# Attention and phase mixing on one core: one PSUM tile, finer loads and phase steps, a new order of all steps

## Chip, core and metric

One core of a Trainium2 chip. The metric is the device time of one execution in microseconds (us); less is better. Steps are issued in a hand-given order, and each engine (PE for products, DVE, ACT and POOL for elementwise work, SP for plain transfers) takes its instructions in that order.

## The reference, cut to what matters

```
scores = q @ k.T / sqrt(64), masked          # 4 batches, 8 heads, 768 positions, 64 wide
                                             # heads 0,2,6: causal; others: 4 sinks + window of 64
x      = softmax(scores) @ v                 # heads side by side: x is (4, 768, 512)
theta  = x @ w_theta
y      = w_tok_r @ (x*cos(theta)) + w_tok_i @ (x*sin(theta))   # over positions, per batch
u      = x + y
out    = u + max(u @ w_ch, 0)
```

## The kernel before

The program is the text `ORDER` (line 54): 732 steps, each a name with arguments, run one after the other by the table `run` (line 435). The framework puts in the waits from the program order and from what the steps read and write; within one engine the order is that of the text.

Per batch b: `lq` (line 206) has POOL load all of q or all of k into `qb`/`kb` as bf16; batch 0 comes through `lf` (line 201, SP) by pair of heads and is cast by `cf`. `tq` (line 225) turns a pair with six (batch 0) or twelve transposes on PE, `eq` copies the result out of PSUM into `qT`/`kT`. `s` (line 254) makes scores of one of 17 units, mostly two halves of up to 512 columns in two PSUM banks; `e` (line 299) is one exponential on ACT over both banks; `m` masks in SBUF on DVE. `av` (line 350) multiplies with v, `n` (line 365) divides on DVE and gives x. x is turned by PE and a copy in batch 0 (`xp`, `xe`), by a transposing transfer on SP later (`xd`). `th` (line 395) makes theta of two row blocks at once, `tr` (line 401) takes cosine and sine of it on ACT into `ct`/`st`, `z` (line 406) multiplies x by one of them: part r mostly both blocks in one DVE instruction of 1024 columns (y = 2), part i one block each, on DVE or POOL. `mx` (line 413) adds four products to the bank of one of six output blocks; three `mx` with p = 0, 1, 2 in that order complete a block. `u` adds x, `ud` turns u by a transfer, `ch` (line 424) makes the last product, `o` (line 428) finishes, `st` stores.

PSUM is four tiles of two banks (line 144). A step that needs one bank gets half of a tile (`one`), a step that needs two gets a whole tile (`two`), so that the two banks of a pair always begin at an even number. `ct`/`st`, `u`, `ot` and the loaded blocks `wtok` take their buffers round robin by their own number. `gv` (line 213) is a small DVE copy that holds the loads of v back.

```
banks = [psum.tile([128, 2, 512], F32, name=f"bank{n}") for n in range(4)]   # line 144
```

Of the kernel before, what the change touches and what calls it, by code (L numbers as in the profile page):

```python
# [57 lines left out]
tq.0.q.3.1 ko.0.1.D lq.1.k sv.0.D e.0.1.4 s.0.6.2 cv.0.1.D lq.1.q eq.0.q.3.1.D eq.0.k.3.0.A s.0.7.4 lw.t e.0.7.4 m.0.1 s.0.5.0 cv.0.2.D lt.0.0 e.0.5.0
m.0.12 s.0.4.4 e.0.6.2 s.0.15.0 bv.0.2.D lt.0.1 m.0.7 e.0.2.6 m.0.5 s.0.3.2 ko.0.3.P m.0.6 e.0.4.4 s.0.14.6 lt.1.0 m.0.2 cv.0.3.D bv.0.0.A lt.1.1
s.0.16.4 m.0.4 e.0.14.6 lt.2.0 cv.0.4.D e.0.16.4 s.0.9.6 bv.0.4.D lt.2.1 e.0.9.6 s.0.8.4 m.0.16 bv.0.3.P e.0.8.4 s.0.13.6 m.0.9 e.0.3.2 m.0.8 e.0.13.6  # L60
m.0.3 tq.1.k.0.4 tq.1.k.3.5 bv.0.1.A m.0.13 av.0.1.2 eq.1.k.0.4.A av.0.2.6 n.0.1.2 eq.1.k.3.5.A tq.1.k.2.4 e.0.15.0 n.0.2.6 av.0.3.2 eq.1.k.2.4.A
ko.1.3.D tq.1.k.1.5 n.0.3.2 cv.0.5.A xp.0.1.0 lq.2.k xp.0.2.1 av.0.0.6 xe.0.1.0.A m.0.15 xp.0.3.4 eq.1.k.1.5.A n.0.0.6 ko.1.2.P av.0.5.2 xe.0.3.4.A
ko.1.1.P tq.1.q.2.0 xe.0.2.1.A n.0.5.2 tq.1.q.0.4 eq.1.q.2.0.A xp.0.0.5 eq.1.q.0.4.D tq.1.q.1.1 xe.0.0.5.A av.0.4.6 eq.1.q.1.1.A xp.0.5.0 n.0.4.6
th.0.0.2 xe.0.5.0.A wt.0.0.0 tq.1.q.3.1 lt.3.0 th.0.1.4 eq.1.q.3.1.D lq.2.q tr.0.0.2 wt.1.0.1 wt.1.1.6 wt.0.1.7 we.1.0.1.A we.1.1.6.D z.0.0.i.0.P
wt.2.0.2 xp.0.4.3 we.0.1.7.D tr.0.1.4 xe.0.4.3.D wt.2.1.1 we.2.0.2.D lt.3.1 th.0.2.6 z.0.0.i.1.D lt.4.0 z.0.0.r.2.D we.0.0.0.A lt.4.1 we.2.1.1.A
s.1.13.2 z.0.1.r.2.D lt.5.0 s.1.1.4 mx.0.0.0.0 tr.0.2.6 z.0.1.i.1.P z.0.1.i.0.D mx.0.2.0.1 lt.5.1 mx.0.0.1.0 z.0.2.r.2.D z.0.2.i.1.P s.1.9.6
mx.0.2.1.1 e.1.1.4 lw.c e.1.9.6 z.0.2.i.0.P m.1.1 s.1.12.4 e.1.12.4 m.1.9 wt.3.0.6 mx.0.0.2.0 e.1.13.2 m.1.12 we.3.0.6.A s.1.8.4 m.1.13 s.1.16.2
mx.0.2.2.1 u.0.0.0 e.1.8.4 ud.0.0 s.1.7.6 e.1.16.2 u.0.2.1 s.1.5.0 tq.2.q.3.4 m.1.8 e.1.5.0 tq.2.q.2.5 ud.0.2 e.1.7.6 s.1.2.2 m.1.16 wt.3.1.0 gv.1
tq.2.k.1.1 m.1.5 e.1.2.2 lv.1.2 we.3.1.0.D s.1.4.6 eq.2.q.3.4.A m.1.7 lv.1.0 s.1.0.2 tq.2.q.1.0 lv.1.5 e.1.0.2 m.1.2 mx.0.1.0.4 lv.1.1 lv.1.3 e.1.4.6
m.1.0 s.1.11.2 lv.1.4 mx.0.1.1.4 e.1.11.2 m.1.4 s.1.6.6 mx.0.1.2.4 e.1.6.6 wt.5.0.2 cv.1.2.A u.0.1.4 wt.4.1.3 s.1.15.6 bv.1.2.P lv.2.2 we.5.0.2.D  # L70
we.4.1.3.A tq.2.k.2.4 m.1.6 ud.0.1 tq.2.k.3.2 e.1.15.6 mx.0.3.0.3 eq.2.k.2.4.D cv.1.0.A wt.5.1.6 eq.2.k.3.2.D eq.2.q.2.5.A ko.2.2.P lv.2.0 mx.0.3.1.3
we.5.1.6.A bv.1.0.P sv.1.D ko.2.3.P s.1.3.4 m.1.15 mx.0.3.2.3 e.1.3.4 s.1.14.6 cv.1.5.A u.0.3.3 mx.0.5.0.2 eq.2.q.1.0.A lv.2.5 m.1.3 ud.0.3
eq.2.k.1.1.A av.1.0.4 cv.1.1.D mx.0.5.1.2 n.1.0.4 e.1.14.6 lv.2.1 ko.2.1.P av.1.1.0 bv.1.1.D xd.1.0 mx.0.5.2.2 n.1.1.0 av.1.2.4 cv.1.3.D xd.1.1
u.0.5.2 ch.0.2.3 bv.1.3.A cv.1.4.D lv.2.3 av.1.3.6 n.1.2.4 bv.1.4.P lv.2.4 wt.4.0.2 ud.0.5 o.0.2.3 s.1.10.0 we.4.0.2.A ch.0.1.4 n.1.3.6 xd.1.2
e.1.10.0 mx.0.4.0.5 o.0.1.4 xd.1.3 av.1.4.2 st.0.1 st.0.2 av.1.5.6 n.1.4.2 ch.0.3.4 cv.2.0.A n.1.5.6 xd.1.4 cv.2.5.A bv.2.0.P mx.0.4.1.5 cv.2.1.D
xd.1.5 sv.2.P o.0.3.4 th.1.0.0 cv.2.2.D lv.3.1 st.0.3 lv.3.5 bv.2.2.P mx.0.4.2.5 lv.3.0 cv.2.3.P cv.2.4.D lv.3.2 bv.2.1.P ch.0.0.4 lv.3.3 u.0.4.5
bv.2.4.P tr.1.0.0 lv.3.4 bv.2.3.P ch.0.5.2 o.0.0.4 ud.0.4 th.1.1.6 o.0.5.2 st.0.0 st.0.5 z.1.0.r.2.D z.1.0.i.1.P tq.2.q.0.0 tr.1.1.6 z.1.0.i.0.D
tq.2.k.0.1 lq.3.q th.1.2.4 eq.2.k.0.1.D lq.3.k eq.2.q.0.0.A z.1.1.i.1.D z.1.1.i.0.P mx.1.0.0.1 tr.1.2.4 z.1.1.r.2.D s.2.7.2 s.2.0.6 s.2.5.0 mx.1.0.1.1
z.1.2.r.2.D z.1.2.i.1.P mx.1.1.0.4 mx.1.2.0.5 z.1.2.i.0.P e.2.7.2 mx.1.1.1.4 e.2.5.0 m.2.7 e.2.0.6 mx.1.2.1.5 m.2.5 m.2.0 mx.1.1.2.4 s.2.10.2 u.1.1.4
s.2.11.6 e.2.10.2 mx.1.2.2.5 ud.1.1 e.2.11.6 mx.1.0.2.1 u.1.2.5 ud.1.2 s.2.9.2 u.1.0.1 s.2.4.4 e.2.9.2 s.2.13.6 mx.1.3.0.0 ud.1.0 e.2.4.4 m.2.9  # L80
mx.1.5.0.1 e.2.13.6 m.2.4 mx.1.3.1.0 m.2.13 mx.1.5.1.1 s.2.8.2 mx.1.3.2.0 e.2.8.2 s.2.3.4 u.1.3.0 s.2.2.6 s.2.1.2 e.2.3.4 mx.1.5.2.1 m.2.8 ud.1.3
# [427 lines left out]
```

## Time and profile before

| what | us |
|---|---|
| median of 3 runs (lowest, highest) | 209.87 (208.6, 210.0) |
| span of the profiled execution, first to last instruction | 208.0 |
| PE busy, share of the span | 170.2, 82% |
| DVE busy | 137.7, 66% |
| ACT busy | 123.7, 59% |
| POOL busy | 55.8, 27% |

The profiled execution has no time of its own beside its span; the runs are 0.6 to 2.0 us above the span. An engine's busy time counts each instruction from start to modelled end, so products that overlap in the pipeline make PE look fuller than it is: its pace is read from how many products start in a stretch.

### The profile page before, as it was taken

How to read it: one execution, taken by the hardware profiler on the slowest of the kernel's cores; microseconds unless marked ns; L12 is line 12 of the kernel's file. 1: busy time of each engine (PE TensorE's matmuls, PEld its weight loads, DVE VectorE, ACT ScalarE, POOL GpSimd, SP SyncE). 2: the span in 40 equal slices, each digit the busy share in tenths (PEclk: the TensorE clock that was granted, in tenths of full speed). 3: DMA queues.
4: the chain of work that ended last, by engine and by line, in shares of the span. 5: the costliest groups of instructions: out<-in, count | busy, mean ns of one | idle time of the engine just before them, and what ended most of it. 6: DMA issues, size and time to landing. Idle time of an engine off the chain costs nothing.

```text
span 208.0 us, 4245 instructions
## 1 busy us (share of the span) xinstructions
PE 170.2 (82%) x1707; PEld 94.0 (45%) x1728; DVE 137.7 (66%) x255; ACT 123.7 (59%) x147; POOL 55.8 (27%) x80
## 2 busy tenths in 40 slices
...
GB/s 196 340 225 156 199 205 208 171 92 202 145 95 196 187 157 159 208 174 186 188 173 199 110 31 127 159 87 50 15 54 111 50 129 150 34 71 76 58 144 151
DMA packets 61938, 29.49 MB, mean 142 GB/s; under 512 B 48096, under 2 KB 58848, under 8 KB 61920
## 3 DMA queue, kind: packets, MB, share of 16 engines
...
## 4 chain that ended last, share of the span: by engine, by line
PE 46%; DVE 20%; DMA 12%; ACT 12%; issue 5%; SPq 2%; POOL 0%; DVEq 0%; ACTq 0%; POOLq 0%
PE bank L416 19%; DMA uT<-u 8%; PE bank L426 8%; ACT P L306 5%; PE bank L363 5%; DVE u L422 4%; PE bank L276 4%; PE bank L399 4%; DMA early<-in_q_dram 3%; DVE ot L429 3%; PE bank L232 3%; DVE kT L238 2%; DVE zr L411 2%; DVE early L411 2%; ACT kT L236 2%
## 5 line engine op out<-in xcount | busy, mean ns | idle before, releaser
L306 ACT ACTIVATE P<-bank 128x1024 bf16<-128x1024 f32 (+2 forms) x64 | 57.3, 948 | 15.5 <-PE bank L276 15.5
L426 PE MATMUL bank<-w_ch_sb,uT 128*128 128x512 bf16 x91 | 23.8, 379 | 5.6 <-DMA uT<-u 1.8
L416 PE MATMUL bank<-zr,wtokTr 128*128 128x512 bf16 x67 | 25.5, 381 | 3.5 <-DVE zr L411 1.1
L328 DVE TENSOR_TENSOR P<-P,m_stream 128x1024 bf16<-128x1024 bf16 (+3 forms) x36 | 21.0, 587 | 10.1 <-ACT P L306 9.8
L416 PE MATMUL bank<-early,wtokTi 128*128 128x512 bf16 x71 | 26.9, 379 | 0.3 <-issue 0.2
L276 PE MATMUL bank<-qT,kT 64*128 64x128 bf16 (+3 forms) x240 | 23.0, 271 | 4.7 <-DVE kT L238 1.7
L416 PE MATMUL bank<-early,wtokTr 128*128 128x512 bf16 x68 | 25.7, 379 | 1.1 <-ACT qT L236 0.4
L416 PE MATMUL bank<-zi,wtokTi 128*128 128x512 bf16 x69 | 26.1, 379 | 0.5 <-issue 0.3
L429 DVE SCALAR_TENSOR_TENSOR ot<-bank,u 128x512 f32<-128x512 f32 x24 | 16.1, 687 | 14.5 <-PE bank L416 6.8
L416 PEld LDWEIGHTS <-wtokTr 128*128 128x128 bf16 x144 | 14.0, 97 | 18.8 <-issue 3.5
L416 PEld LDWEIGHTS <-wtokTi 128*128 128x128 bf16 x144 | 14.0, 98 | 16.7 <-issue 3.8
L363 PEld LDWEIGHTS <-P 128*128 128x128 bf16 x472 | 17.2, 101 | 3.2 <-ACT P L306 0.4
L276 PEld LDWEIGHTS <-kT 64*128 64x128 bf16 x240 | 11.6, 100 | 13.9 <-issue 13.1
L403 ACT ACTIVATE ct<-bank,half_pi 128x1024 f32<-128x1024 f32 x12 | 13.4, 1116 | 7.5 <-PE bank L399 4.8
L411 POOL TENSOR_TENSOR early<-early,st 128x512 bf16<-128x512 bf16 x6 | 9.1, 1516 | 32.6 <-ACT st L404 32.5
L363 PE MATMUL bank<-vt,P 128*128 128x65 bf16 x372 | 17.8, 198 | 0.0
L426 PEld LDWEIGHTS <-uT 128*128 128x128 bf16 x96 | 8.5, 97 | 16.7 <-issue 3.8
L238 POOL COPY kO<-kT 128x320 bf16<-128x320 bf16 (+3 forms) x18 | 7.9, 466 | 26.8 <-DVE kT L238 23.1
L238 POOL COPY vo<-vt 64x384 bf16<-64x384 bf16 (+1 forms) x13 | 8.4, 656 | 22.6 <-ACT vt L236 17.2
L422 DVE TENSOR_TENSOR u<-early,bank 128x512 bf16<-128x512 bf16 x12 | 8.1, 686 | 9.3 <-PE bank L416 8.2
L276 PE MATMUL bank<-qT,kO 64*128 64x128 bf16 x100 | 11.4, 233 | 2.1 <-ACT P L306 2.1
L399 PE MATMUL bank<-w_theta_sb,xT 128*128 128x512 bf16 x46 | 11.3, 380 | 2.2 <-DMA xT<-x 1.3
...
## 6 DMA issues: line engine op xcount, KB each, us to landing
...
```

The costliest lines, as they stand in the source:

```text
L238: (nc.vector if eng == "D" else nc.gpsimd).tensor_copy(o, i)
L276: nc.tensor.matmul(*mms[g], start=True, stop=True, skip_group_check=True)
L306: nc.scalar.activation(o, two(bank)[:, :, :o.shape[2]], AF.Exp, scale=scale)
L328: nc.vector.tensor_tensor(o, o, mk, ALU.mult)
L363: nc.tensor.matmul(o, l, r, start=(m == 0), stop=True, skip_group_check=True)
L399: nc.tensor.matmul(two(bank)[:, y], xT[b % 2][:, kk, i * 128:(i + 1) * 128], w_theta_sb[:, kk], start=(kk == 0), stop=(kk == KD - 1))
L403: nc.scalar.activation(ct[n], two(bank), AF.Sin, bias=half_pi)
L411: (nc.vector if eng == "D" else nc.gpsimd).tensor_tensor(z[b % 2][:, i], x[b % 2][:, i], s, ALU.mult)
L416: nc.tensor.matmul(one(bank), wtokT[n][:, s, t * 128:(t + 1) * 128], z[b % 2][:, s], start=(s == 0 and n == 0), stop=(s == NB - 1 and n == ...
L422: nc.vector.tensor_tensor(u[ui(b, t)], x[b % 2][:, t], one(bank), ALU.add)
L426: nc.tensor.matmul(one(bank), uT[ui(b, t)][:, kk], w_ch_sb[:, kk], start=(kk == 0), stop=(kk == KD - 1))
L429: nc.vector.scalar_tensor_tensor(ot[(NB * b + t) % OT_BUFS], one(bank), 0.0, u[ui(b, t)], ALU.max, ALU.add)
```

## The change

- `banks` becomes one PSUM tile of eight banks; `one` and `two` are slices of it, and a pair of banks may begin at any number.
- `lq` loads one pair of heads: 24 transfers that write 192 KB in place of 6 that write 768 KB. They stand in the order behind the turns that free their part of `qb`/`kb`, which is now laid out by pair in all batches.
- `tr` becomes `tc` (cosine) and `ts` (sine), which can stand apart. `z` does one block of 512 columns always: 12 instructions of 1024 columns on DVE and 24 of 512 (11 DVE, 13 POOL) become 48 of 512 (30 DVE, 18 POOL).
- `pw` (10 steps, 20 products of 384 columns of ones into banks that are free) stand among the first loads, turns and scores of batch 0. A memset of `plain` on DVE goes ahead of the other constants.
- The three `mx` of a block may come in any order; the first one of them starts the bank.
- Buffers of `ct`, `st`, `u`, `uT`, `ot`, `wtok` are given out in the order of first use. `gv` is gone.
- The order of all steps is new (783 steps). Copies out of PSUM: `we` from 7 on ACT and 5 on DVE to 1 and 11, `xe` from 5 and 1 to 2 and 4, `eq` from 19 and 13 to 20 and 12. `cv` goes from 8 ACT, 13 DVE, 3 POOL to 10, 6, 8; `ko` puts 3 on ACT.

```diff
-    banks = [psum.tile([128, 2, 512], F32, name=f"bank{n}") for n in range(4)]
+    plain = new("plain", [128, 384])
+    banks = psum.tile([128, 8, 512], F32, name="banks")
     def one(bank):
-        return banks[bank // 2][:, bank % 2]
+        return banks[:, bank]
     def two(bank):
-        return banks[bank // 2]
+        return banks[:, bank:bank + 2]
...
+        nc.vector.memset(plain, 1.0)
...
-        nc.gpsimd.dma_start(out=t, in_=a[b].rearrange("h (p j) d -> p h (j d)", p=128))
+        h0, h1 = PAIRS[n]
+        nc.gpsimd.dma_start(out=t[:, 2 * n:2 * n + 2], in_=a[b, h0:h1 + 1:2].rearrange("h (p j) d -> p h (j d)", p=128))
...
+    def slot(kind, key, count):
+        seen = taken.setdefault(kind, {})
+        return seen.setdefault(key, len(seen) % count)
...
+    def cosine(b, g, bank):
+        nc.scalar.activation(ct[slot("ct", (b, g), TRIG_BUFS)], two(bank), AF.Sin, bias=half_pi)
+    def sine(b, g, bank):
+        nc.scalar.activation(st[slot("st", (b, g), TRIG_BUFS)], two(bank), AF.Sin)
     def phase(b, g, part, y, eng):
...
+        i = 2 * g + y
+        (nc.vector if eng == "D" else nc.gpsimd).tensor_tensor(z[b % 2][:, i], x[b % 2][:, i], t[:, y], ALU.mult)
...
+    def spare(n, bank):
+        for _ in range(n):
+            nc.tensor.matmul(one(bank)[:, :384], plain[:, :128], plain, start=True, stop=True, skip_group_check=True)
```

The new order begins and ends so (the rest is as new as this):

```
pw.12.1.0 lf.k.0 lf.q.0 pw.5.3.2 pw.14.1.0 lf.k.1 lf.k.2 pw.1.1.6 lf.q.2 cf.k.0.A pw.7.1.0 lf.q.3 lv.0.1 pw.6.3.4 lf.k.3 tq.0.k.0.0 lf.q.1 cf.q.0.D
eq.0.k.0.0.D tq.0.q.0.2 eq.0.q.0.2.A pw.3.3.0 pw.4.3.5 s.0.12.4 lv.0.0 s.0.10.2 e.0.10.2 cf.k.2.D pw.9.3.6 cf.k.1.P tq.0.k.1.6 eq.0.k.1.6.D s.0.2.1
...
o.2.5.6 mx.3.5.0.1 st.2.1 z.3.2.i.0.P st.2.5 mx.3.0.1.6 z.3.2.i.1.D z.3.2.r.1.D mx.3.5.2.1 mx.3.5.1.1 mx.3.1.2.4 u.3.1.4 mx.3.3.2.5 u.3.3.5 ud.3.1
mx.3.4.2.0 u.3.4.0 mx.3.0.0.6 mx.3.0.2.6 u.3.0.6 ud.3.3 u.3.5.1 ud.3.4 mx.3.2.1.4 mx.3.2.2.4 mx.3.2.0.4 u.3.2.4 up.3.5.7 ch.3.1.3 ue.3.5.7.A ch.3.5.4
o.3.5.4 st.2.2 ud.3.0 ud.3.2 ch.3.3.1 ch.3.0.2 o.3.1.3 st.3.5 st.3.1 o.3.3.1 st.3.3 o.3.0.2 ch.3.2.3 st.3.0 o.3.2.3 st.3.2 ch.3.4.6 o.3.4.6 st.3.4
```

## Rows read from the trace of the kernel before

**Rows 1.** Windows by stage: busy us (x instructions) of each engine, PEclk, DMA share, GB/s

```profile
core 0: us, PE busy (x) PEld busy (x) DVE busy (x) ACT busy (x) POOL busy (x), PEclk, DMA share, GB/s
0.00:10.00 10.00, 2.30 (x18) 1.75 (x18) 3.77 (x12) 5.08 (x6) 3.25 (x11) 1.00 0.79 263
10.00:20.00 10.00, 7.40 (x69) 5.13 (x68) 8.47 (x18) 6.64 (x9) 4.29 (x5) 1.00 0.96 211
20.00:25.00 5.00, 2.59 (x32) 1.56 (x32) 4.07 (x11) 4.95 (x8) 4.64 (x9) 0.74 1.18 174
25.00:33.00 8.00, 6.94 (x114) 5.97 (x112) 5.10 (x13) 7.70 (x11) 1.04 (x2) 0.52 1.25 204
40.00:100.00 60.00, 52.20 (x542) 28.48 (x550) 42.07 (x71) 44.46 (x53) 26.04 (x33) 1.00 0.87 163
100.00:186.00 86.00, 77.23 (x740) 39.54 (x750) 61.56 (x109) 49.08 (x56) 14.44 (x17) 1.00 0.52 101
203.50:208.00 4.50, 0.00 (x0) 0.00 (x0) 0.98 (x2) 0.00 (x0) 0.00 (x0) 0.85 0.46 175
```

**Rows 2.** Chain of waits, start and length in us: pieces where PE ran without a stop

```profile
43.99 1.02 PE bank L390 x18
59.70 0.79 PE bank L232 x24
98.00 5.35 PE bank L416 x24
154.24 0.49 PE bank L276 x10
166.94 2.28 PE bank L363 x75
```

**Rows 3.** Timeline of the first ten microseconds: start, length, instruction, idle before it

```profile
4.64 1.68 DVE L195 MEMSET vo<- 64x1950 bf16 x1 [0.33 <-issue]
9.32 0.82 PE L229 MATMUL bank<-ident,qb 128*128 128x128 bf16 x6 [1.70 <-POOL qb L238]
10.08 1.03 PE L276 MATMUL bank<-qT,kT 64*128 64x512 bf16 x6
```

**Rows 4.** Line 411 by form: count, min/median/max ns

```profile
L411 POOL TENSOR_TENSOR zi<-x,st x7: 1165/1598/1670, 43.7 to 142.6; 128x512 bf16<-128x512 bf16 x7
L411 DVE TENSOR_TENSOR zr<-x,ct x6: 1210/1878/2411, 47.4 to 143.7; 128x1024 bf16<-128x1024 bf16 x6
L411 DVE TENSOR_TENSOR zi<-x,st x5: 677/680/694, 46.8 to 145.2; 128x512 bf16<-128x512 bf16 x5
```

**Rows 5.** Groups by line and form, POOL's issues of loads: busy us, mean ns

```profile
L208 POOL DMA_DIRECT2D kb<-in_k_dram x3 | 2.8, 946 | 10.1 <-PE bank L232 7.3 <-PE bank L229 2.8
L221 POOL DMA_DIRECT2D wtok<-in_moe_w_tok_r_dram x6 | 3.3, 548 | 5.9 <-PE bank L390 5.9
```

**Rows 6.** Timeline: waits between the two banks of one PSUM tile

```profile
6.83 0.80 PE L229 MATMUL bank<-ident,kb 128*128 128x128 bf16 x6 [1.04 <-ACT qT L236]
81.21 1.04 PE L426 MATMUL bank<-w_ch_sb,uT 128*128 128x512 bf16 x3
83.64 0.69 DVE L429 SCALAR_TENSOR_TENSOR ot<-bank,u 128x512 f32<-128x512 f32 x1 [1.12 <-PE bank L416]
```

**Rows 7.** Groups by line and form: readers of PSUM, and one of its writers

```profile
L429 DVE SCALAR_TENSOR_TENSOR ot<-bank,u 128x512 f32<-128x512 f32 x24 | 16.1, 687 | 14.5 <-PE bank L416 6.8 <-PE bank L426 4.1 <-ACT kT L236 1.1
L403 ACT ACTIVATE ct<-bank,half_pi 128x1024 f32<-128x1024 f32 x12 | 13.4, 1116 | 7.5 <-PE bank L399 4.8 <-DVE zr L411 1.4 <-DVE early L411 1.0
L306 ACT ACTIVATE P<-bank 128x768 bf16<-128x768 f32 x16 | 12.9, 818 | 2.5 <-PE bank L276 2.5
L306 ACT ACTIVATE P<-bank 128x1024 bf16<-128x1024 f32 x44 | 43.9, 1026 | 12.9 <-PE bank L276 12.9
L426 PE MATMUL bank<-w_ch_sb,uT 128*128 128x512 bf16 x91 | 23.8, 379 | 5.6 <-DMA uT<-u 1.8 <-DVE kT L238 1.4 <-DVE u L422 1.1
L236 ACT COPY kT<-bank 128x768 bf16<-128x768 bf16 x10 | 7.9, 801 | 3.9 <-DVE qT L238 1.5 <-PE bank L229 0.9 <-PE bank L426 0.8
```

More of the change, by code (lines that the diff above doesn't have):

```diff
@@ L58 @@
[L58 to L81, printed above, removed]
@@ new lines @@
+e.0.14.5 av.0.0.0 tq.1.k.1.2 bv.0.1.D m.0.2 cv.0.2.P n.0.0.0 av.0.1.6 n.0.1.6 e.0.13.3 s.0.16.4 eq.1.k.1.2.A bv.0.2.P m.0.9 e.0.16.4 lq.1.q.0
+tq.1.k.3.6 eq.1.k.3.6.A lq.1.k.0 lw.t tq.1.q.2.2 cv.0.4.A cv.0.3.D bv.0.3.D m.0.13 xp.0.0.7 m.0.16 ko.1.1.A av.0.3.0 n.0.3.0 lq.1.q.3 lt.0.1
+tq.1.k.2.5 lt.0.0 bv.0.4.D xp.0.1.6 xe.0.0.7.D xe.0.1.6.D av.0.2.3 n.0.2.3 eq.1.k.2.5.A av.0.4.0 cv.0.5.P av.0.5.6 lt.2.1 lq.1.q.1 lt.3.0 wt.1.1.3
+eq.1.q.2.2.A xp.0.2.4 wt.2.0.2 n.0.4.0 n.0.5.6 xp.0.4.0 xe.0.2.4.A tq.1.q.0.1 lt.1.0 tq.1.k.0.5 xe.0.4.0.A we.1.1.3.D ko.1.3.A xp.0.5.7 eq.1.q.0.1.D
@@ new lines @@
+ud.0.0 tc.1.1.1 ud.0.2 th.1.2.4 tc.1.2.4 ch.0.3.3 mx.0.4.1.6 ts.1.2.4 o.0.3.3 ko.2.3.D z.1.1.i.1.P z.1.1.i.0.D tq.2.q.1.3 z.1.2.i.1.D ud.0.5
+z.1.1.r.1.P tq.2.k.0.1 lv.2.4 eq.2.q.1.3.A tq.2.q.0.2 lv.2.5 eq.2.k.0.1.D tq.2.k.2.4 ch.0.0.7 eq.2.q.0.2.A o.0.0.7 eq.2.k.2.4.A z.1.2.i.0.P
+z.1.2.r.0.P mx.0.4.0.6 s.2.0.2 s.2.4.4 lq.3.q.1 u.0.4.6 lv.2.1 s.2.8.0 e.2.8.0 ch.0.2.7 cv.2.4.P o.0.2.7 st.0.2 ch.0.5.6 mx.1.0.0.0 ko.2.2.D e.2.0.2
+st.0.0 lq.3.q.3 lv.2.3 e.2.4.4 o.0.5.6 cv.2.0.D s.2.7.1 e.2.7.1 s.2.5.3 e.2.5.3 s.2.12.6 e.2.12.6 s.2.6.4 z.1.1.r.0.P z.1.2.r.1.D mx.1.0.1.0 lq.3.q.2
@@ new lines @@
+mx.1.0.2.0 lq.3.q.0 m.2.12 e.2.6.4 m.2.6 cv.2.1.P u.1.0.0 m.2.4 bv.2.4.D ud.1.0 bv.2.1.P mx.1.5.1.7 s.2.3.1 e.2.3.1 s.2.2.3 e.2.2.3 s.2.10.5
+mx.1.5.0.7 mx.1.5.2.7 u.1.5.7 e.2.10.5 lv.2.2 s.2.16.1 s.2.14.3 cv.2.5.A st.0.3 s.2.1.5 cv.2.3.P e.2.1.5 mx.1.1.0.7 m.2.8 mx.1.1.2.7 e.2.14.3 m.2.3
+m.2.0 av.2.0.5 ud.0.4 m.2.1 lq.3.k.1 lq.3.k.3 lq.3.k.0 n.2.0.5 mx.1.1.1.7 u.1.1.7 mx.1.2.1.3 e.2.16.1 m.2.16 m.2.5 sv.2.P bv.2.0.A s.2.13.4 bv.2.3.D
+e.2.13.4 s.2.15.0 s.2.11.6 mx.1.2.0.3 e.2.15.0 ch.1.0.2 o.1.0.2 cv.2.2.A bv.2.2.P m.2.15 mx.1.2.2.3 m.2.7 lq.3.k.2 av.2.1.0 n.2.1.0 mx.1.3.0.2
@@ new lines @@
+e.2.11.6 xd.2.0 s.2.9.6 u.1.2.3 tq.3.q.1.4 eq.3.q.1.4.D tq.3.k.1.1 st.1.0 ud.1.1 tq.3.k.3.0 ud.1.5 lv.3.4 e.2.9.6 m.2.9 eq.3.k.1.1.A tq.3.k.0.3
+tq.3.q.3.5 eq.3.q.3.5.A tq.3.q.2.6 eq.3.q.2.6.A ud.1.2 tq.3.q.0.1 tq.3.k.2.7 eq.3.k.2.7.A xd.2.1 eq.3.q.0.1.A mx.1.3.1.2 m.2.2 av.2.2.4 m.2.13
+av.2.5.6 eq.3.k.3.0.A eq.3.k.0.3.A n.2.2.4 lv.3.0 mx.1.3.2.2 av.2.3.0 n.2.5.6 av.2.4.3 cv.3.4.P ch.1.1.7 n.2.3.0 xd.2.2 st.0.5 n.2.4.3 o.1.1.7
+th.2.0.0 tc.2.0.0 ko.3.2.P ch.1.5.6 u.1.3.2 o.1.5.6 xd.2.3 ts.2.0.0 th.2.1.3 xd.2.4 xd.2.5 z.2.0.r.0.D cv.3.0.A st.1.1 z.2.0.i.0.D ch.0.4.7 bv.3.4.P
@@ L204, in load_first, with load_qk, tok @@
         nc.sync.dma_start(out=t[:, n], in_=a[0, h0:h1 + 1:2].rearrange("h (p j) d -> p h (j d)", p=128))
-    def load_qk(b, what):
+    def load_qk(b, what, n):
         a, t = (q, qb) if what == "q" else (k, kb)
-        nc.gpsimd.dma_start(out=t, in_=a[b].rearrange("h (p j) d -> p h (j d)", p=128))
+        h0, h1 = PAIRS[n]
+        nc.gpsimd.dma_start(out=t[:, 2 * n:2 * n + 2], in_=a[b, h0:h1 + 1:2].rearrange("h (p j) d -> p h (j d)", p=128))
     def load_v(b, j):
         nc.sync.dma_start(out=st_v[:, j], in_=v[b, :, j * 128:(j + 1) * 128].rearrange("h p d -> p h d"))
-    def hold_v():
-        nc.vector.tensor_copy(st_v[:1, :, 0, 0], wtok[(2 * HOLD[0] + HOLD[1]) % WTOK_BUFS][:1, :NB])
     def load_w(t, src):
         nc.gpsimd.dma_start(out=t, in_=src.rearrange("(ko ki) n -> ki ko n", ki=128))
+    taken = {}
+    def slot(kind, key, count):
+        seen = taken.setdefault(kind, {})
+        return seen.setdefault(key, len(seen) % count)
+    def tok(t, n):
+        return wtok[slot("tok", (t, n), WTOK_BUFS)]
     def load_tok(t, n):
-        nc.gpsimd.dma_start(out=wtok[(2 * t + n) % WTOK_BUFS], in_=(w_tok_r, w_tok_i)[n][t * 128:(t + 1) * 128])
+        nc.gpsimd.dma_start(out=tok(t, n), in_=(w_tok_r, w_tok_i)[n][t * 128:(t + 1) * 128])
     def turn_qk(b, what, n, bank):
@@ L230, in turn_qk @@
                 continue
-            for half, h in enumerate(PAIRS[n]):
-                nc.tensor.transpose(pt[rows(half), j * 128:(j + 1) * 128], t[:, h, j * D:(j + 1) * D], ident)
+            for half in range(2):
+                nc.tensor.transpose(pt[rows(half), j * 128:(j + 1) * 128], t[:, 2 * n + half, j * D:(j + 1) * D], ident)
     def copy(eng, o, i):
@@ L389, in turn_tok @@
         for s in range(NB):
-            nc.tensor.transpose(pt[:, s * 128:(s + 1) * 128], wtok[(2 * t + n) % WTOK_BUFS][:, s * 128:(s + 1) * 128], ident)
+            nc.tensor.transpose(pt[:, s * 128:(s + 1) * 128], tok(t, n)[:, s * 128:(s + 1) * 128], ident)
     def keep_tok(t, n, bank, eng):
@@ L399, in theta, with ti, oi @@
                 nc.tensor.matmul(two(bank)[:, y], xT[b % 2][:, kk, i * 128:(i + 1) * 128], w_theta_sb[:, kk], start=(kk == 0), stop=(kk == KD - 1))
-    def trig(b, g, bank):
-        n = (3 * b + g) % TRIG_BUFS
-        nc.scalar.activation(ct[n], two(bank), AF.Sin, bias=half_pi)
-        nc.scalar.activation(st[n], two(bank), AF.Sin)
+    def cosine(b, g, bank):
+        nc.scalar.activation(ct[slot("ct", (b, g), TRIG_BUFS)], two(bank), AF.Sin, bias=half_pi)
+    def sine(b, g, bank):
+        nc.scalar.activation(st[slot("st", (b, g), TRIG_BUFS)], two(bank), AF.Sin)
     def phase(b, g, part, y, eng):
-        n = (3 * b + g) % TRIG_BUFS
-        z, t = (zr, ct) if part == "r" else (zi, st)
-        i = slice(2 * g, 2 * g + 2) if y == 2 else 2 * g + y
-        s = t[n] if y == 2 else t[n][:, y]
-        (nc.vector if eng == "D" else nc.gpsimd).tensor_tensor(z[b % 2][:, i], x[b % 2][:, i], s, ALU.mult)
+        z, t = (zr, ct[slot("ct", (b, g), TRIG_BUFS)]) if part == "r" else (zi, st[slot("st", (b, g), TRIG_BUFS)])
+        i = 2 * g + y
+        (nc.vector if eng == "D" else nc.gpsimd).tensor_tensor(z[b % 2][:, i], x[b % 2][:, i], t[:, y], ALU.mult)
+    mixed = {}
     def mix(b, t, p, bank):
+        done = mixed[b, t] = mixed.get((b, t), 0) + 1
         for s in (2 * p, 2 * p + 1):
             for n, z in enumerate((zr, zi)):
-                nc.tensor.matmul(one(bank), wtokT[n][:, s, t * 128:(t + 1) * 128], z[b % 2][:, s], start=(s == 0 and n == 0), stop=(s == NB - 1 and n == 1), skip_group_check=True)
+                nc.tensor.matmul(one(bank), wtokT[n][:, s, t * 128:(t + 1) * 128], z[b % 2][:, s], start=(done == 1 and s == 2 * p and n == 0), stop=(done == NB // 2 and s == 2 * p + 1 and n == 1), skip_group_check=True)
     def ui(b, t):
-        return (NB * b + t) % U_BUFS
+        return slot("u", (b, t), U_BUFS)
+    def ti(b, t):
+        return slot("uT", (b, t), U_BUFS)
+    def oi(b, t):
+        return slot("ot", (b, t), OT_BUFS)
     def add(b, t, bank):
```

66 lines of the change are left out of this document (36 added, 30 removed).

## Prediction

> **What bounds the kernel now.** I read the busy table first, then windows by stage, then the chain of waits for PE's pace, then single stretches. In the windows [rows 1] the reader is to see four stages. Up to 10 us almost nothing runs on PE: loads and casts come first. From 10 to 33 us ACT is the fullest engine (6.64 + 4.95 + 7.70 = 19.3 of 23 us), PE is held to its lower level (granted clock 0.74 and 0.52 after a stretch in which it was busy 2.59 of 5 us), and the DMA share is at 1 or above. From 40 to 186 us PE is the bound: busy 52.20 + 77.23 = 129.4 of 146 us, with 16.6 us of gaps. After 203.5 us no product runs any more.
>
> How much of this is work? Stretches without a stop give PE's pace at 2.4 GHz [rows 2]: 5.35/24 = 0.223 us for a 512-column product, 2.28/75 = 0.030 for one with v, 0.49/10 = 0.049 for a score, 0.79/24 = 0.033 for a turn of half a pair, 1.02/18 = 0.057 for a full transpose. There are 480, 472, 340, 288 and 148 of them: 107 + 14.4 + 16.7 + 9.5 + 8.4 = 156 us. The change leaves this sum alone but for 20 spare products. Of the span of 208.0 us, 52 us are therefore time in which PE waits or runs slowly, and a new order can only win from them: some 9 before the first score, some 11 in the ACT-bound stage and its lower clock, 16.6 of gaps from 40 to 186 us, 4.5 after the last product, the rest in short stops and pipeline ends inside busy stretches.
>
> **The change part by part**, against the span of 208.0 us; the median of the runs stands 1.9 us above that.
>
> *Start.* The first score starts at 10.08 us [rows 3]. In the new order k of the first pair is loaded first and cast on ACT as q was; q is cast on DVE, behind all constants. The DVE memset of `vo` ends at 6.32 us, three small ones and that of `plain` follow, so this cast starts near 7 us and its turn near 7.6. The turn takes 0.82 us at PE's lower level, the copy 0.80 [rows 7]: first score at about 9.3 us, if nothing stands ahead of it on PE. But six of the spare products do. One has 384 columns, 0.223 x 384/512 = 0.17 us at the high level and 0.33 at the low one, so six take 1.0 to 2.0 us, of which the copy covers 0.8. First score: 9.4 to 10.5 us. I take no change; ends -0.7 and +0.5. The other 14 (2.3 to 4.6 us) fill time in which PE waits for loads.
>
> *Clock.* What the 20 products may give: six transposes take 0.82 us at 9.32 us [rows 3] against 6 x 0.057 = 0.34 later, so PE is at 1.2 GHz there, whatever the granted clock of 1.00 in that window says. Seven later turns at full pace would save 7 x 0.48 = 3.4 us of PE. But the stage waits for loads and then for ACT, and the dip that the trace shows lies at 20 to 33 us, when the spare products are long over. I take -1 us; ends -4 and 0.
>
> *Loads.* 18 more issues on POOL at 0.55 us each (the price of a `wtok` load, the nearest in size [rows 5]; a whole q or k cost 0.95) are 18 x 0.55 + 6 x (0.55 - 0.95) = 7.5 us more of an engine that is busy 55.8 of 208 us. Each waits for one turn instead of four, so the wait of 7.3 us that stood before a k load goes, but POOL's copies and phase products queue behind the rest. The DMA engines are full to 40 us in any case, so earlier issues there only change which load is late. I take 0; ends -2 and +4 (four batch ends with one 0.95 us issue or wait in the way of a phase step).
>
> *Cosine, sine, phase.* DVE loses 12 instructions of 1024 columns with a median of 1.88 (shortest 1.21) and gains 19 of 512 at 0.68 [rows 4]: 12 x 1.88 = 22.6 against 12.9, 9.7 us less if they run alone. POOL gains 5 at 1.60. On the path this counts only where `mx` waits for the first blocks of a batch, once per batch: a first block is ready after 0.68 instead of 1.21 to 1.88. Four times 0.5 to 1.2 us, of which part is covered by products of the batch before: I take -1; ends -4 and +6 (below, rival 2). The end of the last batch is worse placed: four of its twelve phase steps are on POOL, 4 x 1.6 = 6.4 us, the last two after the last sine. Twelve groups of four products, 0.89 us each (10.7 us), need only blocks 0 to 3 and cover it; without that cover it costs about 2 us.
>
> *Copies out of PSUM.* `we`, `xe`, `cv`, `ko`, `eq` as counted move about 4 us from ACT to DVE and POOL. ACT is short only up to 33 us, where one `cf` more goes off it. Nothing.
>
> *PSUM and order.* In the old program two banks of one tile wait for each other though they share no data [rows 6]: the turn of k into bank 1 waits at 6.83 us for ACT's copy out of bank 0; the `o` of bank 4 starts at 83.64, although its product ended at 81.21 + 1.04 = 82.25, because four products into bank 5 stand before it in the order. Pairs that start anywhere, free buffers, and block parts in any order let the new order put ready products into gaps. Its yield can't be walked step by step; it lies between nothing and the 16.6 us of gaps. What stays in these gaps are turns by DMA and copies with their fixed lengths, so I take half: -8 us.
>
> *Tail.* The last product, finish and store follow each other as before: 0, ends -1 and +1.
>
> Sum: 208.0 - 1 - 1 - 8 = 198 us of span, and with 1.9 us around it **200 us**.
>
> **Rivals.**
>
> *1. One tile means one order (slower, 2 in 10).* Place: every access to PSUM. If waits are kept for the tile as a whole, as both stretches in [rows 6] look for a tile of two banks, then in one tile of eight every exponential, copy and addition waits for all PE steps that stand before it, and PE for all of them. Nothing then overlaps on PSUM: PE's 156 us, 68 exponentials (56.8 for the 60 in [rows 7], 60 with the narrow ones), 24 sines and cosines of about 1.1 (26), 24 each of `u`, `o`, `n`, all taken at the 0.69 of `o` (50), some 45 copies at 0.80 (36), and 153 changes from PE to a reader, each with a pipeline end of about 0.16 us (a product's 0.38 us less its pace of 0.22 [rows 2, 7]; 24): 352 us. [...] It decides as soon as banks that do not touch wait for each other. For it: those rows. Against: in the same trace a phase product is read block by block while later blocks of its tile are still being written, so waits by region exist, and the two halves seen to wait are neighbours that fill their tile; no row shows a wait between banks further apart.
>
> *2. DVE and POOL in each other's way (slower, 18 in 100).* The wide DVE product took 1.21 us at best and 2.41 at worst, 1.20 more, about one POOL product (shortest 1.165) [rows 4]. If the 30 narrow ones meet the 18 on POOL as the wide ones did the 13, each costs up to 2.41/2 = 1.2 us: 36 us of DVE against 22.6 + 11 x 0.68 = 30 before. With loads that hold up POOL in front of its phase steps (+4) and gaps that stay, 208 + 6 + 4 = 218 of span, 220 us. For it: POOL gets both more phase steps and four times the loads. Against: POOL is busy 27%. The Trainium skill (SBUF — State Buffer, "Who interferes with whom") says that a DVE instruction with two inputs in SBUF and a GpSimd instruction that reads SBUF exclude each other for a whole instruction. The spread of 1.20 us agrees; by that rule 18 POOL products could stop DVE for 18 x 1.2 = 21 us, which is more than the 9.7 us that the narrower form gives back.
>
> *3. Nothing gained (11 in 100).* The gaps are set by transposing transfers and copies, the spare products do not raise the clock where it falls, and the order trades one wait for another: 208 to 212 us.
>
> **How the numbers follow.** Forecast 51 in 100, rival 1 20, rival 2 18, rival 3 11. A change within 1% (2.1 us) can't be told from none. The forecast's own range is 190 to 207: 208 - 16.6 - 4 + 1.9 is the most (189), and below 207.8 it is faster. Rival 2 reaches to about 224 with both its ends. A range from 186 to 224 holds the forecast, rivals 2 and 3, and leaves out rival 1, 2 in 10. Faster 0.51, same 0.11, slower 0.38.
>
> **What would show it.** Right: PE busy above 137 us between 40 and 186 us or that stage shorter by some 8 us, `o` and `u` starting within 0.1 us of their own last product, narrow DVE phases near 0.7 us, first score near 10 us. Rival 1: ACT, DVE and PE never busy at once on PSUM work, clock at 0.5 for long. Rival 2: DVE phases of 1 us and more beside POOL ones, POOL busy over 80 us. The forecast is wrong if the gaps from 40 to 186 us stay at 16 us, or if the dip of the clock grows longer than the 13 us it has now.

## The result, and the profile after

The changed kernel takes **191.6 us** (median of 4 runs, 190.8 to 192.1) against 209.2 us (208.4 to 210.0) for the kernel before on the same chip: ratio 0.916, 95% interval 0.912 to 0.920. The forecast was 200, with a range of its own from 190 to 207. Its span is 189.0 us, 19.0 less. Medians are over all executions of a kernel; a ratio leaves out those more than 1.5% above the kernel's fastest, so that a run with one execution left has none.

The page of the kernel after: busy time of three engines, the clock that was granted in 40 slices of 4.7 us, and the chain of waits by engine.

```profile
PE 170.1 (90%) x1748; PEld 94.6 (50%) x1748; DVE 139.8 (74%) x270; ACT 117.0 (62%) x143; POOL 71.7 (38%) x99
...
PEclk9969955999999999999999999999999999999997
...
PE 73%; DVE 8%; DMA 6%; ACT 6%; issue 3%; POOL 1%; SPq 0%; DVEq 0%; POOLq 0%; ACTq 0%
```

The same chain before:

```profile
PE 46%; DVE 20%; DMA 12%; ACT 12%; issue 5%; SPq 2%; POOL 0%; DVEq 0%; ACTq 0%; POOLq 0%
```

PE is as busy as before in microseconds, so the time came out of its idle time: 37.8 us before (208.0 less 170.2), 18.9 now. Its share of the chain rose from 46% to 73%. Windows of the kernel before, in two halves, with the columns of [rows 1]:

```profile
0.00:40.00 40.00, 25.06 (x357) 19.43 (x359) 26.34 (x63) 29.59 (x39) 15.29 (x31) 0.87 1.05 216
40.00:208.00 168.00, 145.15 (x1351) 74.61 (x1370) 111.35 (x192) 94.13 (x109) 40.48 (x49) 1.00 0.62 124
```

And of the kernel after, the same two, one short stretch, and stages of [rows 1]:

```profile
0.00:40.00 40.00, 30.41 (x388) 20.69 (x389) 31.86 (x71) 24.90 (x33) 21.84 (x38) 0.83 1.05 216
40.00:189.00 149.00, 139.65 (x1362) 73.87 (x1359) 107.90 (x200) 92.06 (x110) 49.89 (x61) 0.99 0.73 140
...
10.00:13.00 3.00, 3.00 (x22) 1.60 (x22) 0.37 (x1) 1.74 (x3) 0.00 (x0) 0.51 1.13 320
...
20.00:25.00 5.00, 2.74 (x32) 1.67 (x32) 5.00 (x12) 5.00 (x8) 4.89 (x7) 0.82 1.24 219
25.00:33.00 8.00, 7.13 (x109) 6.06 (x108) 6.79 (x18) 5.17 (x9) 7.89 (x12) 0.50 1.06 176
...
100.00:170.00 70.00, 68.78 (x676) 36.60 (x675) 51.21 (x98) 41.30 (x50) 12.72 (x17) 1.00 0.60 129
...
184.50:189.00 4.50, 0.00 (x0) 0.00 (x0) 1.05 (x2) 0.00 (x0) 0.00 (x0) 0.78 0.53 202
```

Up to 40 us little was won: PE starts 388 products instead of 357, but 20 of them are spare. The clock falls between 20 and 33 us as before, and now also from about 10 to 13 us (granted 0.51), where before it was 1.00 [rows 1]. After 40 us PE idles 149.0 - 139.65 = 9.4 us where it idled 168.0 - 145.15 = 22.9, which is 13.5 us; and it is busy 5.5 us less. Together these are the 19.0 us. Of the 5.5 us some 2 are work that was done before 40 us instead: 11 more of the kernel's own products stand there, and they include seven theta products of 512 columns (an estimate at the prediction's paces). The rest I put down to fewer pipeline ends, since PE stops 8 times after 40 us and stopped 51 times before; that was not measured apart. From 100 to 170 us PE is busy 68.78 of 70 us, so that hardly a gap is left there.

How it runs there, in a stretch of the timeline after (start, length), which answers to [rows 6]:

```profile
129.32 1.04 PE L444 MATMUL banks<-w_ch_sb,uT 128*128 128x512 bf16 x4
...
130.19 0.38 PE L428 MATMUL banks<-zr,wtokTr 128*128 128x512 bf16 x1
...
130.39 0.69 DVE L447 SCALAR_TENSOR_TENSOR ot<-banks,u 128x512 f32<-128x512 f32 x1 [0.44 <-PE banks L444]
```

The four products of `ch` end at 130.36, `o` starts 0.03 us later, and PE is already in another bank. (They are banks 7 and 0, which did not share a tile before either; a case of two neighbours stands at run 4.) Before, in the case of [rows 6], `o` started 1.39 us after its product (83.64 - 82.25). The Trainium skill (PSUM — Partial Sum Buffer, section "PSUM bank collisions raise a hardware error") says that two engines on the same 32 partitions of one bank at once are an error, while accesses to different banks run clean. The stretch agrees: PE writes bank 0 from 130.19 us on, while DVE reads bank 7 from 130.39 to 131.08. So a wait between two banks is the program's own.

The start of the kernel after, answering to [rows 3]:

```profile
7.24 0.56 DVE L248 CAST qb<-early 128x768 bf16<-128x768 f32 x1
...
7.85 0.51 PE L239 MATMUL banks<-ident,qb 128*128 128x128 bf16 x6 [2.15 <-DVE qb L248]
...
8.72 1.30 PE L454 MATMUL banks<-plain 128*128 128x384 bf16 x6 [0.35 <-DVE kT L248]
...
9.95 0.93 PE L286 MATMUL banks<-qT,kT 64*128 64x256 bf16 x8
```

### The profile page after: what moved, and what is told of

The parts are those of the page before. It is cut to its first block, busy times and chain, and to the rows that moved or that the text cites. A ratio compares the mean times of both kernels' runs of the same rounds, so it can differ in the third digit from the quotient of the medians.

```text
span 189.0 us, 4337 instructions
## 1 busy us (share of the span) xinstructions
PE 170.1 (90%) x1748; PEld 94.6 (50%) x1748; DVE 139.8 (74%) x270; ACT 117.0 (62%) x143; POOL 71.7 (38%) x99
## 4 chain that ended last, share of the span: by engine, by line
PE 73%; DVE 8%; DMA 6%; ACT 6%; issue 3%; POOL 1%; SPq 0%; DVEq 0%; POOLq 0%; ACTq 0%
PE banks L428 31%; PE banks L409 10%; PE banks L373 8%; PE banks L444 8%; PE banks L286 7%; ACT P L316 4%; PE banks L242 4%; DMA kb<-in_k_dram 3%; DMA uT<-u 2%; PE banks L400 2%; DVE ot L447 1%; DVE kT L248 1%; DMA out_dram<-ot 1%; PE banks L454 1%; PE banks L390 1%
## 5 line engine op out<-in xcount | busy, mean ns | idle before, releaser
L316 ACT ACTIVATE P<-banks 128x1024 bf16<-128x1024 f32 (+2 forms) x64 | 56.8, 950 | 13.6 <-PE banks L286 12.8
L428 PE MATMUL banks<-early,wtokTr 128*128 128x512 bf16 x72 | 27.4, 380 | 0.7 <-ACT st L415 0.7
L428 PE MATMUL banks<-zr,wtokTr 128*128 128x512 bf16 x72 | 27.4, 381 | 0.0
L428 PE MATMUL banks<-zi,wtokTi 128*128 128x512 bf16 x72 | 27.3, 379 | 0.0
L428 PE MATMUL banks<-early,wtokTi 128*128 128x512 bf16 x72 | 27.3, 379 | 0.0
L444 PE MATMUL banks<-w_ch_sb,uT 128*128 128x512 bf16 x96 | 23.7, 379 | 0.7 <-DMA uT<-u 0.7
L286 PE MATMUL banks<-qT,kT 64*128 64x128 bf16 (+3 forms) x240 | 21.1, 258 | 2.5 <-DVE qT L248 1.7
L447 DVE SCALAR_TENSOR_TENSOR ot<-banks,u 128x512 f32<-128x512 f32 x24 | 16.0, 684 | 9.2 <-PE banks L444 8.3
L373 PE MATMUL banks<-vt,P 128*128 128x65 bf16 x372 | 18.0, 198 | 0.9 <-ACT P L316 0.9
L412 ACT ACTIVATE ct<-banks,half_pi 128x1024 f32<-128x1024 f32 x12 | 13.3, 1114 | 3.4 <-issue 3.3
L415 ACT ACTIVATE st<-banks 128x1024 f32<-128x1024 f32 x12 | 12.3, 1024 | 2.6 <-issue 1.8
```

The source lines that it names most:

```text
L286: nc.tensor.matmul(*mms[g], start=True, stop=True, skip_group_check=True)
L316: nc.scalar.activation(o, two(bank)[:, :, :o.shape[2]], AF.Exp, scale=scale)
L373: nc.tensor.matmul(o, l, r, start=(m == 0), stop=True, skip_group_check=True)
L412: nc.scalar.activation(ct[slot("ct", (b, g), TRIG_BUFS)], two(bank), AF.Sin, bias=half_pi)
L415: nc.scalar.activation(st[slot("st", (b, g), TRIG_BUFS)], two(bank), AF.Sin)
L428: nc.tensor.matmul(one(bank), wtokT[n][:, s, t * 128:(t + 1) * 128], z[b % 2][:, s], start=(done == 1 and s == 2 * p and n == 0), stop=(do ...
```

## Experiments

Two theories stood against each other. **A**: the new order won the time. **B**: the waits between banks of one PSUM tile were the cost, and cutting PSUM otherwise took them away. Times are medians; each ratio is against the kernel before on the same chip.

**1 and 2. Old order, one tile**, run twice.

```diff
-    banks = [psum.tile([128, 2, 512], F32, name=f"bank{n}") for n in range(4)]
+    banks = psum.tile([128, 8, 512], F32, name="banks")
-        return banks[bank // 2][:, bank % 2]
+        return banks[:, bank]
-        return banks[bank // 2]
+        return banks[:, bank:bank + 2]
```

> The kernel before with nothing changed but the PSUM tile: one tile of eight banks in place of four of two; its order, loads, phases and buffers stay. Theory A (the gain of 18 us is the new order's; what banks of one tile wait for each other costs little): 206 to 209 us, `o` of other blocks may start earlier but the products still come in the old order. Theory B (the waits between the two banks of a tile were the cost): at least half of the gain comes alone, 192 to 200 us, and PE's gaps between 40 and 186 us fall below 9 us. Rival 1 of the prediction (everything ordered) would give far over 300 us.

> The kernel before with one PSUM tile of eight banks, again, since its four executions lay between 194.5 and 200.0 us. Expected: median 196 to 200 us, so that the tile alone gives 9 to 13 us of the gain and the new order with its loads, phases and spare products the other 5 to 9.

Measured: 198.7 us (194.5 to 200.0), then 198.6 us (197.6 to 201.3), ratio 0.949 (0.945 to 0.954). Three lines give 10.6 of the 18 us with every step in its old place. B holds for more than half. One of the four executions of run 1 took 194.5 us; why is not known.

PE's idle time shows where the time went. The window after 40 us in run 2, to compare with the two above:

```profile
40.00:196.10 156.10, 143.01 (x1339) 72.47 (x1335) 111.78 (x191) 89.80 (x105) 39.83 (x47) 0.98 0.69 132
```

PE idles 13.1 us there instead of 22.9. The waits of DVE show the kind of wait that went. `o` reads what `ch` made, never what `mx` made. Who waited for `mx` (line 416) in the kernel before:

```profile
who waited for it (us, times):
  DVE u L422: 13.4, 12
  DVE ot L429: 6.8, 3
```

And in run 2, where the wait of `o` is gone:

```profile
who waited for it (us, times):
  DVE u L422: 11.5, 13
```

**3 and 4. New order with even pairs: one tile, then four.** The first gives 431 steps other bank numbers, so that each step with two banks begins at an even one (in the kernel after 46 of 100 begin at an odd one); the second takes back the three lines of runs 1 and 2.

```diff
-th.1.2.4 tc.1.2.4 ch.0.3.3 mx.0.4.1.6 ts.1.2.4
+th.1.2.6 tc.1.2.6 ch.0.3.5 mx.0.4.1.4 ts.1.2.6
```

> The kernel after with other bank numbers: every step that takes two banks now gets an even-numbered pair; order of steps, one tile of eight banks and all else stay. It is the control for the next run. Both theories: 190 to 194 us, as after. If pairs that begin at odd banks are themselves worth something: over 194 us.

> The run before this one (new order, even pairs) with four PSUM tiles of two banks in place of one of eight, and no other edit. Theory A (order): within 2 us of the run with one tile, 190 to 196 us. Theory B (waits between banks of one tile): slower than it by 5 to 12 us, 196 to 204 us, and `u`, `o` and score steps are again seen to wait for a step in the sibling bank.

Measured: 195.9 us (0.932 to 0.943) with one tile, 214.1 us (1.021 to 1.033) with four. The first lies above the 194 us that both theories allowed, so the choice of banks is worth something too (run 9). Between the two it is B again, by 18 us, more than the 5 to 12 expected: with two-bank tiles the new order is slower than the old one. One tile, the view of line 428 (`mx`), what PE's idle time ahead of it ended with (us, times):

```profile
its engine sat idle before it (us, times) until:
  issue: 3.8, 14
  DVE u L440: 0.6, 1
  ACT ct L412: 0.4, 1
```

Four tiles, the same view:

```profile
its engine sat idle before it (us, times) until:
  issue: 11.7, 22
  DVE ot L447: 3.3, 4
  DVE u L440: 2.8, 4
  ACT P L313: 2.0, 2
...
```

The steps, their order and their banks are the same, so the reuse of a bank asks for the same waits in both. Ahead of `mx`, four tiles add waits for `o`, `u` and an exponential, and 7.9 us of idle time that the profile can't name (issue). All of PE's work after 40 us, one tile first:

```profile
40.00:194.60 154.60, 141.64 (x1365) 74.92 (x1363) 107.04 (x202) 92.33 (x111) 49.32 (x61) 1.00 0.74 134
40.00:212.00 172.00, 148.52 (x1449) 79.06 (x1448) 111.28 (x211) 95.72 (x115) 50.35 (x62) 1.00 0.68 124
```

PE idles 13.0 us with one tile and 23.5 with four, much as the old order has 13.1 and 22.9: four tiles cost some 10 us of PE's idle time in either order. The rest of the 18 us arises before 40 us, by which time the run with four tiles has started 86 products fewer (299 against 385). A single case, with four tiles:

```profile
117.92 1.03 PE L444 MATMUL bank<-w_ch_sb,uT 128*128 128x512 bf16 x4
...
118.98 0.69 DVE L447 SCALAR_TENSOR_TENSOR ot<-bank,u 128x512 f32<-128x512 f32 x1 [2.71 <-PE bank L444]
...
119.73 0.38 PE L428 MATMUL bank<-early,wtokTr 128*128 128x512 bf16 x1 [0.78 <-DVE ot L447]
```

and the same steps with one tile:

```profile
107.34 1.03 PE L444 MATMUL banks<-w_ch_sb,uT 128*128 128x512 bf16 x4
...
108.20 0.38 PE L428 MATMUL banks<-early,wtokTr 128*128 128x512 bf16 x1
...
108.40 0.69 DVE L447 SCALAR_TENSOR_TENSOR ot<-banks,u 128x512 f32<-128x512 f32 x1 [1.77 <-PE banks L444]
```

In the order stand `ch.1.0.4 o.1.0.4 ... mx.1.2.2.5`: `ch` and `o` use bank 4, and the `mx` behind them goes on in bank 5, in which it has already added products. With four tiles it waits until `o` is done, 0.78 us; with one it follows the last product of `ch` at once and `o` runs beside it.

**5. Two tiles of four banks**, otherwise as run 3.

```diff
-    banks = psum.tile([128, 8, 512], F32, name="banks")
+    banks = [psum.tile([128, 4, 512], F32, name=f"bank{n}") for n in range(2)]
-        return banks[:, bank]
+        return banks[bank // 4][:, bank % 4]
-        return banks[:, bank:bank + 2]
+        return banks[bank // 4][:, bank % 4:bank % 4 + 2]
```

> The new order with even pairs, PSUM cut into two tiles of four banks. One tile of eight gave 195.9 us, four of two 214.1. Theory B1 (only a bank that shares a tile of two is waited for): 194 to 198 us. Theory B2 (any tile that isn't whole PSUM brings waits; the more banks in it, the more siblings): over 214 us.

Measured: **318.5 us**, ratio 1.526 (1.517 to 1.535). B2: tiles of four banks cost more than tiles of two. The view of line 428:

```profile
its engine sat idle before it (us, times) until:
  issue: 56.0, 92
  ACT P L316: 8.4, 9
  ACT kT L246: 8.2, 2
  DVE u L440: 5.9, 6
...
```

The tile that is the whole of PSUM is the exception among the three cuts. Why its banks are kept apart and those of a part are not, no run shows; it stays open.

**6. No spare products.** The ten `pw` steps and the memset of `plain` are left out.

```diff
-        nc.vector.memset(plain, 1.0)
-pw.12.1.0 lf.k.0 lf.q.0 pw.5.3.2 pw.14.1.0 lf.k.1 lf.k.2 pw.1.1.6 ...
+lf.k.0 lf.q.0 lf.k.1 lf.k.2 ...
```

> The kernel after without its 20 spare products and the memset that feeds them. By the forecast (they fill time in which PE waits, six of them stand before the first score): 190.5 to 192.6 us, as after, with the first score near 9.5 us in place of 9.95. Rival (they hold PE's clock up in the stage to 20 us): turns and scores up to 20 us run at 0.5 more often and the time is 193 to 196 us.

Measured: 190.3 us (189.1 to 191.5), ratio 0.906 to 0.918: not told apart from after. Clock and two rows of the start:

```profile
PEclk9999999999999999999999999999999999999999
...
7.45 0.82 PE L237 MATMUL banks<-ident,qb 128*128 128x128 bf16 x6 [1.71 <-DVE qb L246]
...
9.16 0.93 PE L284 MATMUL banks<-qT,kT 64*128 64x256 bf16 x8 [0.89 <-ACT qT L244]
```

The spare products do speed up one turn (0.51 us in the kernel after, 0.82 here) and make the first score 0.8 us later. Nor do they keep the clock up: the kernel after has its second dip (0.51 from 10 to 13 us) with them, and without them the clock stayed at 2.4 GHz right through this execution. In the profiled executions of runs 10, 11 and 12, which leave them out as well, the granted clock of the first 20 us is 1.00, against 0.91 in the kernel after. But the execution with the full clock took 191.3 us, and the fastest of the four, 189.1 us, had the lowest mean clock (0.97). So the dips cost nothing that shows in the time.

**7. Loads by single head.** Twice the transfers at the same places.

```diff
-        nc.gpsimd.dma_start(out=t[:, 2 * n:2 * n + 2], in_=a[b, h0:h1 + 1:2].rearrange("h (p j) d -> p h (j d)", p=128))
+        for y, h in enumerate((h0, h1)):
+            nc.gpsimd.dma_start(out=t[:, 2 * n + y:2 * n + y + 1], in_=a[b, h:h + 1].rearrange("h (p j) d -> p h (j d)", p=128))
```

> The kernel after with every load of q or k of batches 1 to 3 cut once more, by single head: 48 transfers of 96 KB in place of 24 of 192 KB, at the same places in the order. It adds 24 issues to POOL (0.5 us each by a load of `wtok`, 12 us) and no bytes. If an issue on POOL is off the path, as the prediction's term of 0 has it: 190.5 to 193 us. Rival (POOL is what the finer loads cost, 7.5 us of issues already in after): 194 to 200 us, with phase products on POOL starting later.

Measured: 191.0 us (0.908 to 0.920). 24 more issues on POOL do not move the time: they are off the path. This doubles the finer loads rather than undoes them; whole loads have no place in the new order, which turns one pair before another is loaded.

**8. Wide cosine products.** The two `z` of part r of a block pair become one.

```diff
-z.1.0.r.1.D ts.1.0.3 ... z.1.0.r.0.D
+z.1.0.r.2.D
...
+        i = slice(2 * g, 2 * g + 2) if y == 2 else 2 * g + y
+        s = t if y == 2 else t[:, y]
```

> The kernel after with the 24 products by the cosine put back as 12 of 1024 columns on DVE, each where the second of its two stood; 12 of them leave POOL. By the prediction's term (the split gives 1 us): 191.5 to 194 us, DVE busy up by 8 to 13 us, POOL down by 15. Rival (the split with its half on POOL is what frees PE's operands in time): 195 to 200 us, with idle time of PE ahead of `mx` put down to these products. Other rival (POOL and DVE in each other's way): 188 to 190.5 us.

Measured: 191.7 us (0.913 to 0.922). The split is worth nothing here. DVE busy was 140.1 us (139.8 in after), not 8 to 13 more; POOL fell by 16. One group of line 420 in the kernel after (min/median/max ns):

```profile
L420 DVE TENSOR_TENSOR early<-early,st x8: 676/1164/1648, 78.7 to 168.1; 128x512 bf16<-128x512 bf16 x8
```

and with wide cosine products:

```profile
L420 DVE TENSOR_TENSOR early<-early,st x8: 677/688/1649, 80.2 to 168.5; 128x512 bf16<-128x512 bf16 x8
```

With 12 products gone from POOL, these eight of the 18 sine products on DVE fall from a median of 1.16 us to 0.69; the other ten had 0.68 already. In the trace of the kernel after, the 14 narrow products on DVE with no POOL instruction at work beside them all took 0.68 to 0.69 us, and the other 16, beside one, up to 1.65. So the engines do hold each other up, and while PE is the bound it does not show in the time.

**9. Other banks, any pair.** Bank numbers by the rule of run 3, but with 30 of the 100 pairs at odd banks.

```diff
-th.1.2.4 tc.1.2.4 ch.0.3.3 mx.0.4.1.6 ts.1.2.4
+th.1.2.2 tc.1.2.2 ch.0.3.7 mx.0.4.1.0 ts.1.2.2
```

> The kernel after with its banks given out anew by the rule that made the run with even pairs (long rest of each bank between two uses), but pairs may begin at any bank: 30 of 100 begin at an odd one. Order and the rest as in after. If even pairs themselves cost the 4.3 us between after (191.6) and the run with even pairs (195.9): 190.5 to 192.5 us. If it is the choice of banks, whatever the pairs: 194 to 197 us.

Measured: 193.4 us (0.918 to 0.928), between the two expectations. Free pairs give 2.6 us over even ones by the same rule; the banks chosen in after may give 1.8 more, but these two intervals touch.

**10 and 11. Constants on POOL**, on top of run 6; run twice.

```diff
-        nc.vector.memset(vo[:64], 0.0)
+        nc.gpsimd.memset(vo[:64], 0.0)
...
-eq.0.k.0.0.D
+eq.0.k.0.0.A
```

(The two small memsets of `vo` move too.)

> An attempt to be faster: no spare products (190.3 us), the memsets of `vo` (1.84 us ahead of the cast of q on DVE) moved to POOL, which idles from 4 to 7.6 us, and the first copy of k from DVE to ACT, which idles then too. If the start counts: first score near 7.8 us in place of 9.16 and 188.5 to 189.3 us. If loads bound the stage to 40 us: first score earlier, and 190 to 191 us all the same.

> The run without spare products, with the memsets of `vo` on POOL and the first copy of k on ACT, again with more rounds: 189.28 us before (0.9088 of the kernel before, 0.9037 to 0.9139), against 191.6 (0.9159, 0.9119 to 0.9198) for the kernel after. If it is really faster than after: 188.5 to 189.8 us with a ratio below 0.912 at the upper end. If the two are the same: 190 to 192 us.

Measured: 189.3 us, then **188.9 us** (187.4 to 190.3), ratio 0.903 (0.897 to 0.908), below the interval of the kernel after. Its start in the second run:

```profile
3.62 1.72 POOL L197 MEMSET vo<- 64x1950 bf16 x1
...
5.27 0.56 DVE L246 CAST qb<-early 128x768 bf16<-128x768 f32 x1 [0.95 <-DMA early<-in_q_dram]
...
7.60 0.93 PE L284 MATMUL banks<-qT,kT 64*128 64x256 bf16 x8 [0.89 <-ACT qT L244]
```

The cast of q now waits for its load instead of a memset, and the first score comes 2.35 us earlier than in after. This is the fastest version of the study. Its interval still touches that of run 6 alone (0.906 to 0.918), so how much each of the three edits gives stays open.

**12. `wtok` turned by transfers**, on top of run 10: six `wt` and `we` pairs become steps that call `turn` on SP.

```diff
-wt.3.0.5 we.3.0.5.D
+wd.3.0
...
+        "wd": lambda t, n: turn(wtokT[int(n)][:, :, int(t) * 128:(int(t) + 1) * 128], tok(int(t), int(n))),
```

> The run with the constants on POOL (189.3 us, PE busy 68.6 of 70 us from 100 to 170 us) with six of the twelve turns of `wtok` (blocks 3, 4, 5) taken from PE and given to transposing transfers on SP. It takes 36 transposes (36 x 0.057 = 2 us) from PE and 6 copies from DVE. If PE is the bound after 40 us now: 186.5 to 188 us. Rival (the DMA engines, at a share of 0.90 from 40 to 100 us, are the bound there, and `mx` or `xd` waits for transfers): 189 to 194 us.

Measured: 196.8 us (0.936 to 0.946), slower. The rows are of an execution of 199.4 us, so they name the wait and not its price:

```profile
PEld L426 <- DMA wtokTi<-wtok: 6.7, 1, 6.7
```

One turn of `wtok` arrived so late that `mx` waited 6.7 us at once. The transfer stands in SP's queue among loads of v and turns of x, which have to pass there too. Whether that queue is the cause, and whether a better place would save it, was not tried.

## Why the prediction was right, and where it was mis-sized

The time moved the way the forecast had it, and in its main term for the reason it gave: banks that share no data no longer wait for each other. 191.6 us lies near the low end of the forecast's own range, because that term was taken at less than half of what it gave.

- **PSUM and order (-8).** The mechanism was right and the size was not: the span fell by 19.0 us, and after 40 us. I took half of the 16.6 us of gaps as likely and all of it as the most. Gaps gave 13.5. The other 5.5 came out of what counts as busy: some 2 are work moved ahead of 40 us, and for the rest I had listed "short stops and pipeline ends" and then left them out of the bound. I also put the gain on the order, with the tile as what lets it. The runs turn this round: the tile alone gives 10.6 us in the old order, and the new order (with even pairs) without it costs 5.5 (214.1 against 208.5). The sign that I named for it, `o` and `u` within 0.1 us of their own last product, came for 15 of 24 `u` but only 7 of 24 `o` in the kernel after (run 2: 16 and 14). Late readers remain, then; what fell is PE's own idle time. The other sign came: PE is busy 139.65 us between 40 and 186 us, above 137.
- **Rival 1 (one tile means one order).** Its mechanism exists, which two tiles of four banks show at 318.5 us, but not in the tile of eight banks: 198.6 us in the old order. Its counter-argument, that waits by region exist, held there. [Rows 6] could not tell the two apart, and why the whole tile escapes was not found; that a range without this rival held is partly luck.
- **Start (0).** First score at 9.95 us, inside 9.4 to 10.5. q's cast on DVE behind the constants set it, and six spare products, which waited for k's copy and ran from 8.72 us on. Run 11 starts its first score 2.35 us earlier; 0.8 of them came with leaving the spare products out (run 6), the rest with the constants and k's copy moved.
- **Clock (-1).** Wrong by its size: run 6 gives 0, an end of the range. The dip between 20 and 33 us stayed and one of some 3 us at 10 to 13 us came on top. So the lower level lasted longer in all, some 14 us against some 10, which comes close to a sign of being wrong that I had named (a longer dip); the time does not show it. The price was off too: I took 0.82 - 0.34 = 0.48 us for a turn at the lower level, but 0.34 leaves out the pipeline's end. At the high level a turn takes 0.51, so it is 0.31.
- **Loads (0).** Right on the path, by run 7. But an issue costs 0.75 us, not the 0.55 I took: 9.0 + 8.9 = 17.9 us of POOL by the two groups below this list. The wait ahead of k loads in [rows 5], 10.1 us, is 0.0 now.
- **Cosine, sine, phase (-1).** Run 8, which takes back the cosine half, gives 0. The 30 narrow DVE products take 25.6 us (9.0 + 7.8 + 4.7 + 4.1 by group), not the 30 x 0.69 = 20.6 of an undisturbed one. I also took too much for the wide ones: 1.88 us is the median of the six in [rows 4]; the other six have 1.33, and all twelve took 20.1 us, not 22.6.
- **Rival 2 (220 us).** The rule that I cited from the Trainium skill (SBUF — State Buffer, "Who interferes with whom") agrees with the traces: beside POOL products 0.68 us becomes up to 1.65. But the 30 products came to 25.6 us, not to the rival's 36, POOL stayed at 71.7 us, under the 80 that I had named as its sign, and DVE, busy 74%, has room for the 5 us of stretching. The other sign, DVE products of 1 us and more beside POOL ones, did come.
- **Tail (0).** 4.5 us from the last product to the end, as before.
- **Copies (0).** Not tried alone.
- **Rival 3 (nothing).** The gaps did not stay: PE's idle time after 40 us fell from 22.9 us to 9.4, of which some 4.6 are the tail in both.

The loads in the kernel after, busy us, mean ns and idle time before them:

```profile
L213 POOL DMA_DIRECT2D kb<-in_k_dram x12 | 9.0, 752 | 0.0
...
L213 POOL DMA_DIRECT2D qb<-in_q_dram x12 | 8.9, 745 | 0.0
```

What the tile does not explain of the gain, 198.6 to 191.6, is left to the new order with its free pairs, buffers and banks. No single part of it but the banks was found to be worth over 1%; the buffers, the copies and the free order of the three `mx` were not tried alone.
